# The attention front of a fused attention and gated-MLP kernel, written out as a list of small steps pinned on every engine

## Chip, core and metric

The kernel runs on one core of a Trainium2 chip. The metric is the device time of one execution in microseconds (us). The engines are TensorE (PE; its weight loads are PEld), VectorE (DVE), ScalarE (ACT), GpSimd (POOL) and SyncE (SP, which here only issues DMAs). Each engine runs its own instructions in the order in which they stand in its program, and waits on semaphores for the others.

## What is computed

```python
def _attn_ref(q, k, v):                 # q, k, v: (8, 8, 576, 64)
    scores = scale * np.matmul(q, k.transpose(0, 1, 3, 2))
    mask = (rel >= 0) & (rel < 64)      # sliding window of 64
    scores = np.where(mask, scores, -1000000000.0)
    attn = softmax(scores)              # max subtracted, sum + 1e-09
    return np.matmul(attn, v)
def _moe_ref(x, w_gate, w_val, w_out):  # x: (4608, 512), d_ff 1536
    gate = 1.0 / (1.0 + np.exp(-(x @ w_gate)))
    return (gate * (x @ w_val)) @ w_out
```

The attention output, heads side by side, is the x of the second function.

## The kernel before

The 4608 tokens are cut into 12 tiles of 384. A tile's attention is worked in four **units** (t, p): t is the tile's place in the order of work, p a pair of heads. A unit has two halves h, and in each three pieces u of 128x128. The path of a unit is:

- `load_qk`, `load_v`: three DMAs of 192, 224 and 384 KB.
- `scores` (s): 24 small matmuls (L224).
- `exponentials`: for each of six pieces, DVE adds the mask and takes the row's lowest value (L249), ACT takes the exponential (L257), for h = 0 with its row sum.
- `normalize`: for h = 1 DVE sums the rows (L270). DVE doubles the sum (L264) and inverts it (L265), POOL multiplies the half by it (L274).
- `stage_b`: three transposes on PE (pp, L328) and a copy by ACT (pT, L333) for each half.
- `stage_c`: 24 matmuls with v (oo, L358), then `x_split`: ACT writes the rounded x (L365), DVE the rest that rounding lost (L366).

Weights come from HBM as 64-bit words of 512 KB a block and are turned to float32 on the chip: **conv** i, with i = 3 j + m, where m is 0 for the gate, 1 for the value and 2 for the output weights. `conv_load` is the DMA into one of 6 raw buffers; `conv_a` is two ACT steps (L117 into one of 3 w32 buffers, L118); `conv_b` is three DVE steps (L126, L128, L130); `conv_c` is ACT's rounding (L158), DVE's rest (L159) and the stores for later use, among them the w32 buffer itself (L154). A w32 buffer is free for the next conv once L159 is done and that store has landed.

The MLP of tiles 0 and 1 is `up(t, j, 0)` (gate), `up(t, j, 1)` (value), 12 matmuls each (L394): for each p three products, of w rounded and x rounded, w rounded and x's rest, w's rest and x rounded. A `ph` result lies in one of three PSUM banks, taken in turn. ACT's tanh (L402) empties the gate's bank, DVE's product (L407) the value's; L420 and L422 split the hidden value, and `down` (L442, 9 matmuls for a j) adds it up. The order is up(0,0), up(1,0), up(0,1), down(0,0), up(1,1), up(0,2) and so on. From t = 2 on, another attention unit is put in about every 12 us. Later tiles use products of summed blocks (L619), of which most of the time consists.

The order within an engine comes from two things. The kernel's lines are put on a list of events with due times (`put`, sorted near the end), and PE's matmuls are kept in the order of that list (`pe`). On the other engines the scheduler of the framework picks the order; `issue_after(x)` puts an instruction behind x on the same engine, without a wait when it runs.

Of the kernel before, what the change touches and what calls it, by code (L numbers as in the profile page):

```python
# [26 lines left out]
def attn_ffn(ctx: ExitStack, tc: tile.TileContext, qT, kT, vN, w_gate, w_val, w_out, out, outT):  # L27
# [74 lines left out]
    def conv_load(i):  # L102
        j, m = divmod(i, KINDS)
        raw = mp.tile([P, DM], I64, name=f"raw_{m}_{j}", tag="raw", bufs=RAW)
        marks["conv_load"] = nc.sync.dma_start(out=raw, in_=w_src[m][J_AT[j]]).ins
        conv[i] = raw

    def conv_a(i):


        j, m = divmod(i, KINDS)
        raw = conv[i]
        hw = raw.bitcast(F32).rearrange("p (n two) -> p n two", two=2)[:, :, 1]
# [3 lines left out]
        nc.scalar.activation(w32, hw, AF.Copy, scale=2.0 ** -112)  # L117
        nc.scalar.activation(r32, lw, AF.Copy, scale=2.0 ** -29)  # L118
        conv[i] = (r32, w32)

    def conv_b(i):
        j, m = divmod(i, KINDS)
        r32, w32 = conv[i]
        wi = w32.bitcast(I32)
        zz = mp.tile([P, DM], I32, name=f"zz_{m}_{j}", tag="u", bufs=2)
        nc.vector.tensor_scalar(out=zz, in0=wi, scalar1=4, scalar2=1,  # L126
                                op0=ALU.logical_shift_left, op1=ALU.logical_shift_right)
        nc.vector.scalar_tensor_tensor(out=wi, in0=wi, scalar=-2 ** 31, in1=zz,  # L128
                                       op0=ALU.bitwise_and, op1=ALU.bitwise_or)
        nc.vector.tensor_add(out=wi, in0=wi, in1=r32)  # L130

    def conv_c(i):
        j, m = divmod(i, KINDS)
        _, w32 = conv.pop(i)
# [7 lines left out]
        J = J_AT[j]  # L142
        if m == 2:
            w2 = w2.rearrange("p a b h -> p a (b h)")
            hi, lo = wo[j] = w2[:, 0, :], w2[:, 1, :]
            cp = split(w32, hi, lo, nc.vector)
            wo_all[j] = w2
            wo_parts(j)
        else:
            cp = split(w32.rearrange("p (a h) -> p a h", a=2), w2[:, :, 0, :], w2[:, :, 1, :], nc.vector)  # L150
            wgv[m][j] = w2
            for name, half in (("A11", 0), ("A12", 1)) if J < NK else (("A22", 1),):
                put_part(m, J % NK, name, w2[:, half])
# [12 lines left out]
    def load_qk(t, p):
# [10 lines left out]
        nc.sync.dma_start(out=qt, in_=qT[rows, c0:c0 + TT])  # L180
        nc.sync.dma_start(out=kt, in_=kT[rows, c0:c0 + TT + BLK])
        ld[(t, p)] = (qt, kt)

    def load_v(t, p):
        i = 8 + 4 * t + p
# [5 lines left out]
        nc.sync.dma_start(out=vt, in_=vN[r0:r0 + P, :].rearrange("p (u c) -> p u c", u=UT))  # L191
# [20 lines left out]

    def scores(t, p, starts=(True,) * (2 * UP)):
# [15 lines left out]
    def softmax(t, p):  # L229
        sc = sc_of.pop((t, p))  # L230
        for h in range(2):
            exponentials(t, p, h, sc[h])
            normalize(t, p, h)

    def exponentials(t, p, h, sc):
        g0 = order[t] * UT
# [85 lines left out]

    def stage_b(t, p):
        for h in range(2):
            pt = st[(t, p, h)]
            pp = bank(t, p, f"p{h}", f"pp{h}_{t}_{p}")
            for u in range(UP):
                pe(nc.tensor.transpose(pp[:, u, :], pt[:, u, :], ident))  # L328
            if t < 2:
                pT = mp.tile([P, TT], F32, name=f"pT{h}_{t}_{p}", tag="g", bufs=4).rearrange("p (u c) -> p u c", u=UP)  # L330
            else:
                pT = pt
            cp = nc.scalar.copy(pT, pp)  # L333
            marks["pTv"] = cp.ins
            if t < 2:
                marks["pT"][NP * t + p] = cp.ins
            st[(t, p, h)] = pT

    def stage_c(t, p):
        oo = bank(t, p, "o", f"oo_{t}_{p}")  # L340
        outputs(t, p, [oo[:, u, :] for u in range(UP)])
        oo = oo.rearrange("p u c -> p (u c)")
        if t < 2:
            xs[(t, p)] = x_split(oo, f"{t}_{p}", 4 * t + p, nc.vector)
        else:
            marks["xf"] = nc.scalar.copy(xf_tile(t, p), oo).ins
# [59 lines left out]
    def gated(out, val, g):  # L406
        nc.vector.scalar_tensor_tensor(out=out, in0=g, scalar=1.0, in1=val, op0=ALU.add, op1=ALU.mult)  # L407

    def up_gate(t, j):
        gate_table(t, j, up(t, j, 0))  # L410

    def hidden_split(t, j, h32, eng):
# [7 lines left out]
        nc.vector.tensor_copy(out=h_hi, in_=h32)  # L420
        hh[(t, j)] = (h_hi, h_lo)
        return eng.tensor_sub(out=h_lo, in0=h32, in1=h_hi.bitcast(F32))  # L422

    def up_val(t, j):
        ph = up(t, j, 1)
        g = gates.pop((t, j))
        h32 = mp.tile([P, TT], F32, name=f"h32_{t}_{j}", tag="c", bufs=CB)
        gated(h32, ph, g)
        last = hidden_split(t, j, h32, nc.vector)
        if t == 0:  # L430
            marks[j] = (marks["gate"], last.ins)

    def down(t, j, i, first, last):
# [46 lines left out]
    def put_part(m, k, name, parts):  # L480
        nc.sync.dma_start(out=wd[k][N_OF[name]][:, m], in_=parts.bitcast(F32))
# [319 lines left out]
    for i, (kind, t, j) in enumerate(plan):  # L801
# [31 lines left out]
    def last_tile(t, js):  # L833
# [5 lines left out]
        for n, (j, x) in enumerate(items):  # L839
# [3 lines left out]
            put(now, 9, down, t, j, x, j == js[0], j == js[-1])  # L843
# [111 lines left out]
    events.sort(key=lambda x: (x[0], x[1]))  # L955
    for tm, _, f, a in events:
        if f in (conv_a, conv_b, conv_c):
            with ExitStack() as behind:
# [5 lines left out]
                key = j - AHEAD if m < 2 else j - 1  # L964
                early = {3: ("1_1",), 2: ("1_3",), 4: ("1_3",), 5: ("1_3",)}.get(a[0], (key,))
# [54 lines left out]
```

## Time and profile before

| | before |
|---|---|
| three runs | 946.29, 947.2, 947.6 us, median 947.2 |
| the profiled execution | span 945.2 us from first to last instruction; the median of the runs is 2.0 us more |
| PE busy | 930.8 us, 98% of the span |
| DVE, ACT, POOL busy | 713.7 (76%), 501.7 (53%), 151.2 us (16%) |

The span is the time between the first and the last instruction of one profiled execution. A busy PE isn't one at its peak: matmuls are pipelined and their ends modelled. Times below count from the start of the span. The **front** is the stretch up to about 40 us, in which the eight units of tiles 0 and 1 are worked and the first weights turned.

### The profile page before, as it was taken

To read this page: it belongs to the slowest core of one execution; us is meant where nothing else is said; L and a number is where in the kernel's file an instruction comes from. 1 tells how busy PE (TensorE), PEld (TensorE's weight loads), DVE (VectorE), ACT (ScalarE), POOL (GpSimd) and SP (SyncE) were. 2 spreads that over 40 slices of the span, in tenths; PEclk is the share of its full clock that TensorE was granted. 3 is DMA by queue.
4 is the path that set the end of the run, shared out by engine and by line. 5 is a ranking of instruction groups with operands and counts; after the bars stand their busy time and mean duration, and the time that the engine had idled before them with its cause. 6 is when DMAs were issued, how large, how long until landed. Compare 5 with 4: busy or idle time off the path is not lost.

```text
span 945.2 us, 20293 instructions
## 1 busy us (share of the span) xinstructions
PE 930.8 (98%) x7164; PEld 897.2 (95%) x7164; DVE 713.7 (76%) x1919; ACT 501.7 (53%) x1374; POOL 151.2 (16%) x232
## 2 busy tenths in 40 slices
PE   6999999999999999999999999999999999999998
PEld 5899999889999999999999999999999999999998
DVE  7999989887888975666885676796567796566882
ACT  7867676655666653545653255564155555222450
POOL 4201104605683000311100013100011100000000
PEclk9999999999999999999999999999999999999999
DMA  9899998989999989888879888889888688988364
GB/s 339 309 386 366 359 320 283 358 295 352 388 321 314 405 284 294 288 273 270 269 251 312 264 283 293 270 244 288 284 278 280 213 246 281 297 251 256 128 222 158
DMA packets 105509, 273.45 MB, mean 289 GB/s; under 512 B 11456, under 2 KB 33600, under 8 KB 105408
## 3 DMA queue, kind: packets, MB, share of 16 engines
q1 hardware_dynamic: 105408, 272.15, 85.2%
q8 instruction: 57, 0.93, 0.4%
q14 instruction: 44, 0.36, 0.1%
HBM read 220.20 MB, written 51.90 MB: 288 GB/s over the span
## 4 chain that ended last, share of the span: by engine, by line
PE 95%; DVE 2%; DMA 1%; ACT 0%; issue 0%; DVEq 0%; ACTq 0%
PE pr L619 46%; PE y L619 23%; PE ph L394 10%; PE y L442 5%; PE pp L328 3%; PE pr L358 2%; PE s L224 1%; PE oo L358 1%; PE pr L224 1%; DMA wt<-wd 1%; PE s L358 1%; DVE p L249 0%; DVE rs L264 0%; ACT p L257 0%; DVE x L366 0%; DVE rs L270 0%
## 5 line engine op out<-in xcount | busy, mean ns | idle before, releaser
L619 PE MATMUL pr<-x_T,wt 128*128 128x384 f32 x1224 | 224.5, 335 | 0.0
L619 PE MATMUL y<-h,wot 128*128 128x384 f32 x1260 | 219.9, 334 | 0.0
L619 PEld LDWEIGHTS y<-h,wot 128*128 128x128 f32 x1260 | 218.3, 188 | 0.7 <-DVE h L407 0.6
L619 PEld LDWEIGHTS pr<-x_T,wt 128*128 128x128 f32 x1224 | 212.6, 188 | 0.3 <-issue 0.3
L619 PE MATMUL pr<-x_B,wt 128*128 128x384 f32 x1008 | 188.6, 337 | 1.0 <-DMA wt<-wd 1.0
L619 PEld LDWEIGHTS pr<-x_B,wt 128*128 128x128 f32 x1008 | 174.6, 188 | 3.5 <-issue 2.1
L701 ACT CAST h<-h 128x384 fp32r<-128x384 f32 x210 | 104.3, 514 | 91.7 <-PE y L619 41.1
L274 POOL TENSOR_TENSOR p<-p,rs 128x384 f32<-128x384 f32 x76 | 69.3, 926 | 521.7 <-DVE rs L265 243.3
L702 DVE TENSOR_TENSOR h<-h,h 128x384 fp32r<-128x384 f32 x210 | 111.7, 559 | 22.0 <-ACT h L701 21.5
L257 ACT ACTIVATE p<-p,mn 128x128 f32<-128x128 f32 x288 | 110.8, 392 | 20.5 <-DVE mn L249 20.2
L402 ACT ACTIVATE g<-c 128x384 f32<-128x384 f32 x90 | 47.0, 522 | 117.7 <-DVE c L658 117.5
L394 PE MATMUL ph<-x,w 128*128 128x384 f32 x576 | 106.0, 338 | 0.1
L394 PEld LDWEIGHTS ph<-x,w 128*128 128x128 f32 x576 | 99.8, 188 | 2.5 <-issue 0.9
L629 DVE TENSOR_TENSOR c<-pr,p 128x384 f32<-128x384 f32 x60 | 33.0, 550 | 44.5 <-PE pr L619 44.5
L407 DVE SCALAR_TENSOR_TENSOR h<-g,c 128x384 f32<-128x384 f32 x90 | 50.3, 559 | 6.2 <-DVE c L658 0.5
L257 ACT ACTIVATION_READ_ACCUMULATOR p<-p,mn 128x1 f32 x264 | 49.6, 188 | 0.0
L333 ACT COPY p<-pp 128x384 f32<-128x384 f32 x80 | 34.3, 479 | 25.9 <-PE pp L328 23.1
L634 ACT COPY p<-pr 128x384 f32<-128x384 f32 x60 | 27.2, 473 | 37.0 <-PE pr L619 36.9
L629 DVE TENSOR_TENSOR u<-pr,p 128x384 f32<-128x384 f32 x60 | 33.1, 551 | 17.6 <-PE pr L619 17.6
L328 PE MATMUL pp<-ident,p 128*128 128x128 f32 x288 | 41.8, 280 | 2.0 <-POOL p L274 1.9
L619 PE MATMUL pr<-x_T,ws 128*128 128x384 f32 x216 | 40.4, 339 | 0.0
L658 DVE TENSOR_TENSOR c<-pr,p 128x384 f32<-128x384 f32 x60 | 32.9, 554 | 9.6 <-PE pr L619 9.1
(186 smaller groups left out, 1212.1 us busy)
## 6 DMA issues: line engine op xcount, KB each, us to landing
wt<-wd SPq DMA_DIRECT2D x186, 512.0 KB, 4.5
wot<-wod SPq DMA_DIRECT2D x105, 512.0 KB, 4.6
v<-in_vN_dram SPq DMA_DIRECT2D x48, 384.0 KB, 5.5
wd<-ws SPq DMA_DIRECT2D x48, 256.0 KB, 4.9
k<-in_kT_dram SPq DMA_DIRECT2D x48, 224.0 KB, 5.5
q<-in_qT_dram SPq DMA_DIRECT2D x48, 192.0 KB, 5.4
w32d<-w SPq DMA_DIRECT2D x36, 256.0 KB, 4.9
wd<-w SPq DMA_DIRECT2D x36, 256.0 KB, 5.5
```

The source lines that it names most:

```text
L257: exp = nc.scalar.activation(pt[:, u, :], pt[:, u, :], AF.Exp, bias=mn[:, u:u + 1], scale=-1.0, **sums)
L274: eng.tensor_mul(out=pt, in0=pt, in1=rs.unsqueeze(2).broadcast_to([P, UP, P]))
L328: pe(nc.tensor.transpose(pp[:, u, :], pt[:, u, :], ident))
L358: pe(nc.tensor.matmul(oo[U // 2][h * BLK:(h + 1) * BLK, U % 2 * BLK:(U % 2 + 1) * BLK], vt[:, U, h * BLK:(h + 1) * BLK], pT[h][:, U // 2, ...
L394: pe(nc.tensor.matmul(ph, l, r, start=i == 0, stop=i == len(prs) - 1))
L402: act = nc.scalar.activation(g, c, AF.Tanh)
L407: nc.vector.scalar_tensor_tensor(out=out, in0=g, scalar=1.0, in1=val, op0=ALU.add, op1=ALU.mult)
L442: pe(nc.tensor.matmul(yb[y], l, r, start=first and n == 0, stop=last and n == 2))
L619: pe(nc.tensor.matmul(ps, l, r, start=first and i == 0, stop=last and i == 2, skip_group_check=not check))
L629: marks["plus"] = nc.vector.tensor_add(out=o, in0=ps, in1=a).ins
L701: nc.scalar.copy(h2[:, 0, :], src)
L702: nc.vector.tensor_sub(out=h2[:, 1, :], in0=src, in1=h2[:, 0, :].bitcast(F32))
```

## The change

The functions of the front are cut into small named steps, and a string, FRONT, lists 330 of them: 49 loads and stores, 36 steps of PE, 98 of ACT, 131 of DVE and 16 of POOL. They are traced in this order before all other events, and each engine keeps exactly this order (`Pinned`, with SP among the engines). A step's name is two letters and its numbers: `lq`, `lv` loads, `sc` scores, `tt` L249, `ex` L257, `rd` L270, `ia` L264, `ib` L265, `mu` L274, `tr` and `cp` transposes and copy, `ou` L358, `xh`, `xl` x rounded and its rest, `ug`, `uv` the two `up`, `ut` tanh, `ud`, `uh`, `ul` L407, L420, L422; and of conv: `cl` load, `ch`, `cw` L117 and L118, `cz`, `cs`, `ca` L126, L128, L130, `cc`, `cr` L158 and L159, `ct`, `cd` stores. The list holds all eight units, up(0,0), up(1,0) but for its value's product, and conv 0 to 7. Steps that the list names are not run again by the events. All other events due before 60 are put behind the last pinned instruction of their engine. Some explicit orders go, such as the exponentials' `issue_after` to a pT copy. No instruction is added or taken away.

```diff
+FRONT = """
+lq0.0 cl0 lq0.1 lq0.2 sc0.0 lq1.0 lq0.3 ch0 tt0.0.0.1 tt0.0.0.2 cw0 lv0.1 tt0.0.0.0 tt0.0.1.1 lv0.0 sc0.1
+tt0.0.1.0 ex0.0.0.0 tt0.0.1.2 lq1.1 ex0.0.0.1 ex0.0.0.2 ex0.0.1.1 ia0.0.0 sc0.2 ib0.0.0 ex0.0.1.2 lq1.3
+tt0.1.0.1 mu0.0.0 tt0.1.0.0 ex0.0.1.0 tt0.1.0.2 ex0.1.0.1 rd0.0.1 ex0.1.0.2 lq1.2 tt0.1.1.0 tr0.0.0 ex0.1.0.0
+tt0.1.1.1 ia0.0.1 tt0.2.0.1 ex0.1.1.0 ia0.1.0 ib0.0.1 ex0.1.1.1 tt0.1.1.2 sc0.3 mu0.0.1 tt0.2.0.0 ex0.2.0.1
+tt0.2.0.2 tt0.2.1.2 lv0.2 ex0.1.1.2 tt0.2.1.0 ex0.2.0.0 ib0.1.0 tt0.2.1.1 tr0.0.1 mu0.1.0 rd0.1.1 cp0.0.0
+sc1.0 lv0.3 ex0.2.0.2 tt0.3.0.2 tt0.3.0.1 ex0.2.1.0 lv1.2 ia0.1.1 tr0.1.0 cz0 cp0.0.1 ou0.0 tt0.3.0.0 lv1.1
...
+ex1.2.1.2 rd1.1.1 cd1 cc1 tt1.3.0.1 cl7 ex1.2.0.0 rd1.2.1 cl5 ex1.2.0.1 tt1.3.0.2 cr1 uv0.0 ch3 lq2.0
+tt1.3.1.0 cw4 ia1.1.1 tt1.3.1.1 ia1.2.0 ia1.2.1 ex1.3.1.1 ib1.1.1 cz3 mu1.1.1 ch4 tt1.3.1.2 cs3 ex1.3.0.1
+ut0.0 tr1.1.1 cz4 cp1.1.0 ib1.2.1 ib1.2.0 ud0.0 cp1.1.1 mu1.2.0 ou1.1 cs4 ex1.3.1.0 ex1.3.1.2 mu1.2.1
+ex1.3.0.2 rd1.3.1 ex1.3.0.0 ia1.3.1 cw3 ia1.3.0 tr1.2.1 ib1.3.0 ib1.3.1 ca4 mu1.3.0 tr1.2.0 cw2 ca3 cd4 xh1.0
+mu1.3.1 ch2 tr1.3.0 xl1.0 cd3 cp1.2.0 cz2 ct1 tr1.3.1 cp1.2.1 cs2 ou1.2 cp1.3.0 cl9 cp1.3.1 ca2 xh1.1 cl10
+ou1.3 cc3 xl1.1 cd2 xh1.2 cr3 cc4 lv2.2 xl1.2 xh1.3 ct3 cw5 xl1.3 ug1.0 cl8 ch6 uh0.0 cr4 cc2 uv1.0 cz6 ch7
+cr2 cw6 cs6 cz7 ca6 ch5 cs7 cl12 cw7 cz5 ut1.0 ul0.0 cc6 cs5 ca7 ca5 cc7 cl13 cr6 cd6 cc5 cd7 cr7 ct2 cr5 cd5
+ct6 lv2.0 ct4 ct7 cl11
+"""
...
+    class Pinned:
...
+                ins = getattr(self.eng, op)(*a, **k)
+                if pinned[0]:
+                    tc.keep_in_program_order(ins)
+                    ends[ins.ins.engine] = ins.ins
+                return ins
...
+    def run(name, *a):
+        if (name,) + a not in taken:
+            taken.add((name,) + a)
+            steps[name](*a)
...
-                if NP * t + p - 2 in marks["pT"] and (t, p) != (1, NP - 1):
-                    behind.enter_context(tc.issue_after(marks["pT"][NP * t + p - 2]))
...
+    pinned[0] = True
+    for token in FRONT.split():
+        run(token[:2], *map(int, token[2:].split(".")))
+    pinned[0] = False
     for tm, _, f, a in events:
...
+            for ins in ends.values() if tm < 60 else ():
+                behind.enter_context(tc.issue_after(ins))
...
-                if a[0] < 2:
-                    behind.enter_context(tc.issue_after(marks["pT"][a[0] + (f is conv_c)]))
```

## Rows read from the trace of the kernel before

**Rows 1.** The head of the page: the span, each engine's busy time, and PE's busy tenths in 40 slices of 23.6 us.
```profile
span 945.2 us, 20293 instructions
PE 930.8 (98%) x7164; PEld 897.2 (95%) x7164; DVE 713.7 (76%) x1919; ACT 501.7 (53%) x1374; POOL 151.2 (16%) x232
PE   6999999999999999999999999999999999999998
```

**Rows 2.** Busy time of the engines by stretch: the sum over 0 to 40.3 us, and the stretch from 40 to 60 us (length, then busy us and instructions of PE, PEld, DVE, ACT, POOL, granted clock as a share of 2.4 GHz, DMA share, GB/s).
```profile
sum 40.30, PE 30.92 PEld 24.95 DVE 31.67 ACT 31.95 POOL 16.45; mean PE 3.86 PEld 3.12 DVE 3.96 ACT 3.99 POOL 2.06
...
40.00:60.00 20.00, 20.00 (x139) 18.90 (x134) 17.77 (x46) 16.07 (x38) 0.00 (x0) 1.00 0.94 332
```

**Rows 3.** The chain that ended last, from 36 to 54 us (start, length, engine, tile and line).
```profile
36.23 1.48 PE pp L328 x12
...
37.79 0.85 ACT pT L333 x2
...
38.69 1.67 PE oo L358 x46
40.37 8.72 PE ph L394 x48
...
51.17 2.11 PE ph L394 x12
53.28 0.82 PE s L224 x24
```

**Rows 4.** The first instructions of PE in order of time (start, length, and in brackets the idle time before and what ended it).
```profile
3.91 1.55 PE L224 MATMUL s<-k,q 64*64 64x128 f32 x24 [3.91 <-DMA k<-in_kT_dram]
6.57 2.84 PE L224 MATMUL s<-k,q 64*64 64x128 f32 x48 [1.11 <-DMA k<-in_kT_dram]
```

**Rows 5.** Two DMA issues of SP, of k for unit (0,1) and of v for (0,0) (start of issue), and under them the same two with size and us from issue to landing.
```profile
2.11 0.43 SPq L181 DMA_DIRECT2D k<-in_kT_dram  x1
...
3.53 0.43 SPq L191 DMA_DIRECT2D v<-in_vN_dram  x1
...
k<-in_kT_dram SPq DMA_DIRECT2D x1, 224.0 KB, 4.3
...
v<-in_vN_dram SPq DMA_DIRECT2D x1, 384.0 KB, 4.9
```

**Rows 6.** DVE and ACT in order of time: the first step of unit (0,1) on each, four ACT steps in a row, and the last x steps of the front.
```profile
8.79 0.28 DVE L249 CUSTOM_DVE_ANT_0 p<-s,m 128x128 f32<-128x128 f32 x1
...
9.12 0.40 ACT L257 ACTIVATE p<-p,mn 128x128 f32<-128x128 f32 x1 [1.03 <-DVE mn L249]
...
18.41 0.61 ACT L158 CAST w<-w 128x512 fp32r<-128x512 f32 x1
...
18.92 0.67 ACT L117 ACTIVATE w<-raw 128x512 f32<-128x512 f32 x1
...
19.49 0.67 ACT L118 ACTIVATE raw<-raw 128x512 int32<-128x512 uint32 x1
...
20.05 0.45 ACT L365 CAST x<-oo 128x384 fp32r<-128x384 f32 x1
...
40.34 0.85 ACT L365 CAST x<-oo 128x384 fp32r<-128x384 f32 x2
...
41.08 1.01 DVE L366 TENSOR_TENSOR x<-oo,x 128x384 fp32r<-128x384 f32 x2
```

**Rows 7.** Busy time of the engines from ACT's first step of unit (0,1) to the end of its last x step (columns as in rows 2).
```profile
9.12:41.19 32.07, 27.71 (x397) 22.19 (x390) 29.11 (x140) 29.21 (x98) 13.19 (x15) 1.00 0.95 357
```

**Rows 8.** DVE's instructions up to 45 us grouped by line (count, busy us, mean ns, idle time before them).
```profile
L264 DVE SCALAR_TENSOR_TENSOR rs<-rs 128x3 f32<-128x3 f32 x16 | 4.5, 280 | 1.0 <-ACT p L257 0.8
...
L130 DVE CUSTOM_DVE_ANT_0 w<-raw,w 128x1024 uint16<-128x1024 uint16 x5 | 3.6, 723 | 0.3
L128 DVE SCALAR_TENSOR_TENSOR w<-w,zz 128x512 int32<-128x512 int32 x5 | 3.4, 688 | 0.1
...
L126 DVE TENSOR_SCALAR zz<-w 128x512 int32<-128x512 int32 x5 | 2.1, 419 | 0.0
```

**Rows 9.** POOL's multiplications and the DVE steps beside them, in order of time.
```profile
17.20 0.69 DVE L130 CUSTOM_DVE_ANT_0 w<-raw,w 128x1024 uint16<-128x1024 uint16 x1
17.31 1.27 POOL L274 TENSOR_TENSOR p<-p,rs 128x384 f32<-128x384 f32 x1 [2.08 <-ACT p L257]
...
26.41 0.83 POOL L274 TENSOR_TENSOR p<-p,rs 128x384 f32<-128x384 f32 x1 [1.64 <-DVE rs L265]
...
26.60 0.65 DVE L264 SCALAR_TENSOR_TENSOR rs<-rs 128x3 f32<-128x3 f32 x1
```

**Rows 10.** Two stores of a w32 buffer (issue, then us from issue to landing), the waits of ACT's L117 for such stores from 41 to 140 us (total, times, longest), and DVE's product of up(1,0).
```profile
26.25 0.33 SPq L154 DMA_DIRECT2D w32d<-w  x1
...
39.81 0.32 SPq L154 DMA_DIRECT2D w32d<-w  x1
...
w32d<-w SPq DMA_DIRECT2D x1, 256.0 KB, 7.0
...
w32d<-w SPq DMA_DIRECT2D x1, 256.0 KB, 3.8
...
ACT w L117 <- DMA w32d<-w: 6.7, 6, 2.9
...
45.42 0.55 DVE L407 SCALAR_TENSOR_TENSOR h<-g,ph 128x384 f32<-128x384 f32 x1
```

More of the change, by code (lines that the diff above doesn't have):

```diff
@@ L117, in conv_a, with cz @@
[L117 to L121, printed above, removed]
+        scalar.activation(r32, lw, AF.Copy, scale=2.0 ** -29)
+        conv[i]["r32"] = r32
+    @step
+    def cz(i):
         j, m = divmod(i, KINDS)
-        r32, w32 = conv[i]
-        wi = w32.bitcast(I32)
+        wi = conv[i]["w32"].bitcast(I32)
         zz = mp.tile([P, DM], I32, name=f"zz_{m}_{j}", tag="u", bufs=2)
[L126 to L130, printed above, removed]
@@ L133, in conv_c, with cc @@
+    @step
+    def cc(i):
         j, m = divmod(i, KINDS)
-        _, w32 = conv.pop(i)
+        w32 = conv[i]["w32"]
         if m < 2 or j < 8:
@@ L211, in pieces, with sc, front_scores @@
         return [b[:, u, :] for u in range(UP)]
+    @step
+    def sc(t, p):
+        scores(t, p)
+    def front_scores(t, p):
+        run("sc", t, p)
     def scores(t, p, starts=(True,) * (2 * UP)):
@@ L229, in softmax @@
     def softmax(t, p):
+        if t < 2:
+            for h in range(2):
+                for u in range(UP):
+                    run("tt", t, p, h, u)
+                    run("ex", t, p, h, u)
+                for name in ("rd",) * h + ("ia", "ib", "mu"):
+                    run(name, t, p, h)
+            return
         sc = sc_of.pop((t, p))
@@ L233, in softmax, with mask_of, lowest @@
             normalize(t, p, h)
-    def exponentials(t, p, h, sc):
-        g0 = order[t] * UT
+    def mask_of(t, u, h):
+        key = [int((order[t] * UT + 2 * u + s) % SEQ == 0) for s in range(2)]
+        return masks[tuple(key[::-1] if h else key)]
+    def lowest(t, p, h):
         if t < 2 and (NP * t + p) % 3 == 2:
@@ L321, in stage_n, with tr, cp @@
             normalize(t, p, h)
+    @step
+    def tr(t, p, h):
+        pt = st[(t, p, h)]
+        pp = pp_of[(t, p, h)] = bank(t, p, f"p{h}", f"pp{h}_{t}_{p}")
+        for u in range(UP):
+            pe(nc.tensor.transpose(pp[:, u, :], pt[:, u, :], ident))
+    @step
+    def cp(t, p, h):
+        pp = pp_of.pop((t, p, h))
+        if t < 2:
+            pT = mp.tile([P, TT], F32, name=f"pT{h}_{t}_{p}", tag="g", bufs=4).rearrange("p (u c) -> p u c", u=UP)
+        else:
+            pT = st[(t, p, h)]
+        marks["pTv"] = scalar.copy(pT, pp).ins
+        if t < 2:
+            marks["pT"][NP * t + p] = marks["pTv"]
+        st[(t, p, h)] = pT
@@ L335, in stage_b, with ou, xh @@
-            if t < 2:
-                marks["pT"][NP * t + p] = cp.ins
-            st[(t, p, h)] = pT
+            run("tr", t, p, h)
+            run("cp", t, p, h)
+    @step
+    def ou(t, p):
+        oo = oo_of[(t, p)] = bank(t, p, "o", f"oo_{t}_{p}")
+        outputs(t, p, [oo[:, u, :] for u in range(UP)])
+    @step
+    def xh(t, p):
+        oo = oo_of[(t, p)].rearrange("p u c -> p (u c)")
+        if t < 2:
+            x2 = xs[(t, p)] = xp.tile([P, 2, TT], F32R, name=f"x_{t}_{p}", tag=f"x{4 * t + p}")
+            marks[f"{t}_{p}"] = (scalar.copy(x2[:, 0, :], oo).ins,)
+        else:
+            marks["xf"] = scalar.copy(xf_tile(t, p), oo).ins
@@ L339, in stage_c, with xl @@
+    @step
+    def xl(t, p):
+        oo = oo_of.pop((t, p)).rearrange("p u c -> p (u c)")
+        x2 = xs[(t, p)]
+        lo = vector.tensor_sub(out=x2[:, 1, :], in0=oo, in1=x2[:, 0, :].bitcast(F32))
+        marks[f"{t}_{p}"] += (lo.ins,)
     def stage_c(t, p):
-        oo = bank(t, p, "o", f"oo_{t}_{p}")
-        outputs(t, p, [oo[:, u, :] for u in range(UP)])
-        oo = oo.rearrange("p u c -> p (u c)")
+        run("ou", t, p)
+        run("xh", t, p)
         if t < 2:
-            xs[(t, p)] = x_split(oo, f"{t}_{p}", 4 * t + p, nc.vector)
-        else:
-            marks["xf"] = nc.scalar.copy(xf_tile(t, p), oo).ins
+            run("xl", t, p)
@@ L419, in hidden_split, with ul, down, dn @@
             h_lo = mp.tile([P, TT], F32R, name=f"hl_{t}_{j}", tag="hl", bufs=3)
-        nc.vector.tensor_copy(out=h_hi, in_=h32)
+        vector.tensor_copy(out=h_hi, in_=h32)
+        hh[(t, j)] = (h_hi, h_lo, h32)
+    @step
+    def ul(t, j):
+        h_hi, h_lo, h32 = hh[(t, j)]
         hh[(t, j)] = (h_hi, h_lo)
-        return eng.tensor_sub(out=h_lo, in0=h32, in1=h_hi.bitcast(F32))
+        lo = vector.tensor_sub(out=h_lo, in0=h32, in1=h_hi.bitcast(F32))
+        if t == 0:
+            marks[j] = (marks["gate"], lo.ins)
     def up_val(t, j):
[L425 to L433, printed above, removed]
+        for name in ("uv", "ud", "uh", "ul"):
+            run(name, t, j)
+    def down(t, j, i):
+        run("dn", t, j, i)
+    @step
+    def dn(t, j, i):
+        first, last = j == 0, j == NF - 1
         h_hi, h_lo = hh[(t, j)]
```

221 lines of the change are left out of this document (156 added, 65 removed).

## The prediction

> **What bounds the kernel now.** Read the head of the page first: PE is busy for 930.8 of 945.2 us, 14.4 us short of the whole, and the only slices below nine tenths are the first and the last [rows 1]. The busy times by stretch then say where the 14.4 us lie: up to 40.3 us PE is busy for 30.92, so 9.4 us are lost there, and from 40 to 60 us it is busy without a gap [rows 2]. Some 5 us are scattered over the other 900. What the front can give is therefore at most 9.4 us, and 3.9 of them pass before the first q and k are there [rows 4]; that leaves 5.5.
>
> The chain tells what ends the front. PE's last attention products follow a copy by ACT, and at 40.37 `up(1,0)` begins, behind which PE never stands still [rows 3]. But `up(1,0)` needs all four x of tile 1, and the last rest of x (DVE, L366) ends at 41.08 + 1.01 = 42.09, just when the tenth of its first twelve matmuls (8.72 / 48 = 0.18 us each [rows 3]) wants it: 40.37 + 9 x 0.18 = 42.0 [rows 3, 6]. So one event is the gate: **the last xl of tile 1, now at 42.09**. PE's work behind it is the same in both kernels, and a shift of the gate is a shift of the end, as long as nothing new stops PE later. In front of the gate PE isn't what is short: between ACT's first step of unit (0,1) and its last x step, 32.07 us, PE has 27.71 us of work, ACT 29.21 and DVE 29.11 [rows 7]. The front is a relay of ACT and DVE, each idle for only some 2.9 us of 32; the first question to the new order is what it adds to them ahead of the gate.
>
> **The change, part by part.** No instruction is added or lost, so only places count. I reckon along ACT, from its first step of unit (0,1) to its last xh, and take DVE's own sum as a bound.
>
> *Start, +0.8 us.* The list puts the raw block of conv 0, 512 KB, second on SP's queue, ahead of q and k of (0,1). k of (0,1) now lands at 2.11 + 4.3 = 6.41, v of (0,0), 800 KB further on, at 3.53 + 4.9 = 8.43: 2.5 us per 1000 KB, so 512 KB cost 1.3 us [rows 5]. The scores of (0,1) start at 6.57 + 1.3 = 7.9 instead of 6.57, and take 1.55 like those of (0,0): 9.4 [rows 4]. On the other side ACT has L117 and L118 of conv 0 ahead of its first exponential, and DVE's `ia0.0.0` waits for three exponentials ahead of `tt0.1.*`; with raw at 6.7 (96 KB behind 6.41), two conv steps of 0.57 each and the exponentials, that gives 9.6. I take 9.6 against 8.79 now, and ACT's step 0.33 behind it as now, 9.9 against 9.12 [rows 6]. Lower bound: the block, of larger rows, costs nothing, 0. What hides the price now is nothing: ACT waits for it (1.03 us idle there already).
>
> *Work moved ahead of the gate, +1.5 us on ACT.* Today L117, L118 and L158 of three convs lie in that stretch. The list has four of each (`cw0` and `ch0` come sooner still, but conv 3 and 4 are whole and conv 2 has its first two). One more of each costs, from start to start, 0.57 (18.92 to 19.49), 0.56 (to 20.05) and 0.51 (18.41 to 18.92), less the 0.1 of a fourth L117 that already reaches into the stretch [rows 6]. On DVE the three steps of conv 4 and of conv 2 come ahead of the last xl: 2 x (0.42 + 0.69 + 0.72) = 3.7 us [rows 8], less the two splitting steps of the hidden value that go behind it, about 1.4 by the nearest rows of that size: +2.3.
>
> *Idle time that goes, -2.9 us.* ACT's idle time is 32.07 - 29.21 = 2.86, DVE's 2.96 [rows 7]. A list dense enough removes all of it; that is the most there is.
>
> *Idle time that comes, +1.3 us.* First, PE is late early: behind the scores of (0,1), at 9.4, the list has s(0,2), a transpose, s(0,3), a transpose, s(1,0), a transpose, oo(0,0) and the transposes of `cp0.1.1`. At 1.55 for 24 matmuls this is done near 17.4, at the later pace (0.82 [rows 3]) about 13; ACT is at that copy at about 16.2. Between 0 and 1.2, I take 0.8: the early pace is the nearer row. Second, `ch4` wants the w32 buffer of conv 0, whose store follows `cr0`, which stands 15 us of DVE work behind 9.6 and some 1.5 us of losses: 26. The store takes 3.8 to 7.0 us [rows 10], with the two ahead of it about 32; ACT is there at about 31.5. I take 0.5 of 0 to 1.5. Such waits are known from later (6.7 us over six [rows 10]); there they hold nobody up.
>
> *Behind the gate, +0.3 us.* From the gate to `up(1,1)` PE has 51.17 - 42.09 = 9.1 us of work [rows 3, 6]. Its bank is free only when DVE's L407 of up(1,0) has run, which is at 45.42 now [rows 10] and which the list leaves out: it has to stand behind the last pinned DVE step. Between xl1.3 and that end lie 16 steps: three whole convs, two L159 and the split, at the durations of rows 8 and 0.08 less from start to start about 8.5, with L407 9.1. The cover is gone: whatever DVE waits for in that tail, PE waits too. Cost 0 to 3.2 (the spread of a store's landing, 3.8 to 7.0, since `ch6` and `ch5` take buffers that conv 3 and 2 must give up [rows 10]); I take 0.3, since the stores' queue has less in it by then, as at 39.81.
>
> *Edits at nothing.* The other moved loads and stores pass SP in an order whose landings lie ahead of need; the dropped `issue_after` costs no wait at run time. DVE's work finished early (conv 5 to 7) gains nothing, since PE has no gap there that it would fill.
>
> **Sum:** 0.8 + 1.5 - 2.9 + 1.3 + 0.3 = +1.0 us, the gate near 42.8 and the span 946.2. With the 2.0 us by which the runs' median stands above this span: 948.2. A change of 0.2% is 1.9 us, about what a measurement of this kernel can tell from none, so this is no change that would show.
>
> **DVE and POOL.** DVE's L264 begun at 26.60, 0.19 us into a POOL multiplication, took 0.65 against a mean of 0.28 and ended with it; the multiplication begun at 17.31 inside a DVE step took 1.27 instead of 0.83 [rows 8, 9]. So a step of one holds up the other. The Trainium skill (SBUF — State Buffer, section "SBUF: two separate sides") says that the two share a port pair under an exclusive lock, which whoever starts first keeps for its whole instruction, and that DVE steps with two SBUF inputs need it. That speaks against this change, since it moves such steps in among the multiplications; the trace agrees in both directions. By that rule the sum would be that of rival C.
>
> **Rivals.** *A, faster.* ACT never idles and the raw block costs nothing at the start: 1.5 - 2.9 = -1.4; and a tighter start of the later tiles takes another 1 of the 5 us that PE loses elsewhere. For it: every engine's order is free of the scheduler's guesses. Against: the extra work on both engines ahead of the gate. About 944.8. Chance 0.20.
>
> *B, slower: PE waits for the bank at up(1,1).* One place, L407 of up(1,0), behind 16 pinned steps. It decides once DVE's tail is more than about 1 us longer than PE's 9.1; at the late landing it gives 1.0 + 2.9 = +3.9, in the middle +2.5: 949.7. Against: stores at that time may land as quickly as at 39.81. Chance 0.15.
>
> *C, slower: DVE is the bound of the front.* Start 0.8, work 2.3, idle -3.0, so +0.1 and whatever DVE loses. Four more conv steps with two SBUF inputs than now stand among the multiplications; POOL is busy 0.41 of the stretch [rows 7], and a hit costs half of 0.83: 0.7. With 2 of the 3 us of idle time still there the gate moves by +2.8: 950.0. It decides from 1.8 us of DVE losses. Chance 0.17.
>
> *D, the order is nearly the old one.* The scheduler's order might be close to the list; then within 0.5 of 947.2. Against: conv 1, 3 and 4 plainly move. It is part of the 0.48 that no change that shows has in all.
>
> **How the numbers follow.** Faster 0.20 (A), the same 0.48 (the sum with its smaller bounds, and D), slower 0.32 (B and C). The likeliest case gives 948.2, by itself 945.8 to 949.0. The range leaves out the better half of A at the bottom and, at the top, B and C where they add up: 944.4 to 951.0.
>
> **What would show it.** In the new profile: the first L249 of (0,1) at about 9.6; ACT's L117 with a wait for a w32 store near 31; the last xl between 42 and 44, and `up(1,0)` beginning at 40.5 to 41.5; a PE wait before `up(1,1)` for DVE's L407 or none; PE's busy time up to the gate as now. The prediction is wrong if the last xl comes before 41 (ACT's work per step is then less than I took, or the idle time is all gone), or if PE shows new gaps of over 2 us behind the gate.

## The result and the profile after

The changed kernel takes 952.3 us (median of six runs, 949.6 to 955.0) against 947.4 for the kernel before beside it: ratio 1.0054, 95% interval 1.0039 to 1.0068. It is slower by some 5 us. The forecast was 948.2, between 944.4 and 951.0.

The head of its page (span; busy time of the engines; PE's busy tenths and granted clock in 40 slices of 23.8 us) has to be held against [rows 1]:

```profile
span 950.5 us, 20265 instructions
PE 930.8 (98%) x7164; PEld 897.2 (94%) x7164; DVE 712.7 (75%) x1919; ACT 501.6 (53%) x1374; POOL 153.1 (16%) x232
PE   6889999999999999999999999999999999999998
...
PEclk9999999999999999999999999999999999999999
```

PE's work is the same 930.8 us, and the span is 5.3 us longer: what came in is idle time, and a little slow clock that the slices are too coarse to show. Two slices have fallen from 9 to 8: the second, 23.8 to 47.5 us, which holds the end of the front, and the third, 47.5 to 71 us, which lies behind it. Most of the loss is in the third, as the starts of PE's matmuls show further down. The chain that ended last, from the gate on (start, length, engine, tile and line; every step of the list is recorded at L125, the helper in `Pinned`, so there one goes by tiles; L568 is `up`, L644 `down`), against [rows 3]:

```profile
41.22 8.18 DMA w32d<-w
...
49.48 0.66 ACT w L125
50.15 0.56 ACT raw L125
50.70 0.38 ACT g L125
...
51.13 3.72 PE ph L568 x12
54.85 2.08 PE y L644 x9
56.93 2.11 PE ph L568 x12
```

Before, PE ran through here without a break. Now the end of the kernel hangs on the store of a w32 buffer, issued at 41.22. The waits from 41 to 100 us (us in total, times, longest) name who is held up:

```profile
ACT w L125 <- DMA w32d<-w: 7.1, 4, 3.9
DVE zz L125 <- ACT w L125: 6.9, 4, 2.9
...
PEld ph L568 <- ACT g L125: 3.6, 1, 3.6
...
PE ph L568 <- ACT g L125: 3.3, 1, 3.3
```

And the timeline from 36 us gives the order on the queue and on the engines:

```profile
39.88 0.65 SPq L125 DMA_DIRECT2D raw<-in_moe_w_gate_dram  x1
...
40.62 0.51 SPq L125 DMA_DIRECT2D raw<-in_moe_w_val_dram  x1
...
41.22 0.41 SPq L125 DMA_DIRECT2D w32d<-w  x1
...
41.29 6.55 PE L568 MATMUL ph<-x,w 128*128 128x384 f32 x36
...
41.75 1.22 DVE L125 TENSOR_TENSOR x<-oo,x 128x384 fp32r<-128x384 f32 x2
...
49.48 0.66 ACT L125 ACTIVATE w<-raw 128x512 f32<-128x512 f32 x1 [3.95 <-DMA w32d<-w]
...
51.13 3.72 PE L568 MATMUL ph<-x,w 128*128 128x384 f32 x12 [3.29 <-ACT g L125]
```

Read it from the bottom. PE wants to begin the value half of `up(0,1)` at 47.84 (41.29 + 6.55). The `ph` banks are taken in turn, so it needs the one that the gate of `up(1,0)` filled, and ACT's tanh (`ut1.0`, tile g) has to empty that. The tanh stands on ACT behind `ch5` and `cw7` of the list. `ch5` wants the w32 buffer of conv 2, whose store `cd2` stands on SP behind `cl9` and `cl10`, two blocks of 512 KB. From issue to landing, of the issues between 40 and 42 us:

```profile
raw<-in_moe_w_val_dram SPq DMA_DIRECT2D x1, 512.0 KB, 8.1
...
w32d<-w SPq DMA_DIRECT2D x1, 256.0 KB, 8.2
```

Before, the store issued at 39.81 landed in 3.8 us [rows 10]. The stretches show why (length; busy us of PE, PEld, DVE, ACT, POOL; granted clock, DMA share, GB/s), first the kernel before, from 36 and 40 us, then the new one:

```profile
36.00:40.00 4.00, 3.33 (x64) 2.89 (x60) 3.59 (x7) 3.31 (x8) 0.83 (x1) 1.00 0.53 204
40.00:45.00 5.00, 5.00 (x38) 4.71 (x33) 4.38 (x9) 5.00 (x11) 0.00 (x0) 1.00 0.74 221
```

```profile
36.00:40.00 4.00, 2.34 (x26) 1.70 (x28) 3.93 (x9) 3.12 (x8) 2.56 (x3) 1.00 0.88 312
40.00:45.00 5.00, 4.89 (x63) 4.73 (x58) 4.69 (x10) 4.75 (x11) 0.00 (x0) 1.00 1.04 345
```

The DMA engines were half idle ahead of the gate; now they are full. The clock behind the wait, by PE's own row of the new kernel (length; busy us; granted clock, DMA share, GB/s):

```profile
50.73:54.15 3.42, 3.02 (x9) 0.50 0.50 136
```

After the 3.29 us in which PE stood, its granted clock is 0.50, the 1.2 GHz level, for 3.4 us, so the twelve matmuls took 3.72 us where twelve take 2.11 in the chain above: 1.6 us more.

By the starts of PE's matmuls in the traces (us; "151st" is the 151st `up` matmul, "product" the first matmul of the summed blocks; one profiled execution of each kernel):

| kernel | up(1,0) | value of up(0,1) | up(1,1) | 151st | product | span |
|---|---|---|---|---|---|---|
| before | 40.30 | 46.85 | 51.01 | 68.38 | 209.07 | 945.2 |
| after | 41.29 | 51.13 | 56.77 | 74.14 | 214.89 | 950.5 |
| e1_store_first | 41.24 | 48.92 | 53.20 | 73.07 | 215.12 | 950.6 |
| e2_tanh_first | 42.84 | 49.20 | 55.99 | 74.99 | 216.08 | 952.0 |
| e3_tanh_rest_first | 41.79 | 48.17 | 53.63 | 71.08 | 212.19 | 947.1 |
| e4_no_tail | 43.28 | 49.64 | 53.80 | 71.17 | 212.95 | 947.8 |
| e5_filled | 41.97 | 48.33 | 52.49 | 69.86 | 212.67 | 947.4 |
| e6_conv_behind | 40.81 | 47.16 | 51.45 | 70.90 | 211.48 | 947.7 |
| e7_start | 41.75 | 48.10 | 52.26 | 69.63 | 211.87 | 948.1 |
| e8_all | 39.23 | 45.60 | 49.89 | 69.28 | 211.55 | 947.4 |
| e12_four_w32 | 41.63 | 48.04 | 52.20 | 69.82 | 214.08 | 951.2 |
| e13_four_w32_no_tail | 42.16 | 48.54 | 52.70 | 70.08 | 214.32 | 952.1 |
| b2_four_w32 | 40.36 | 46.88 | 51.24 | 74.89 | 218.90 | 957.2 |

So of the 5.76 us that the new kernel is behind at `up(1,1)`, 0.99 were there at the gate, 3.29 are the wait and some 1.5 the low clock. By the first product it is 5.82, by the end 5.3: hardly anything moves behind that. The 0.99 is the least certain of these numbers: the lists of the changed kernel, e2, e3 and e4 are the same up to the gate, and yet it came at 41.29, 42.84, 41.79 and 43.28. In e2 and e4, the late ones, PE ran at the low clock for 3.4 us ahead of it.

### The profile page after: what moved, and what is told of

It reads as the page before. It is cut to its first block, busy times and chain, and to the rows that moved or that the text cites. A ratio compares the mean times of both kernels' runs of the same rounds, so it can differ in the third digit from the quotient of the medians.

```text
span 950.5 us, 20265 instructions
## 1 busy us (share of the span) xinstructions
PE 930.8 (98%) x7164; PEld 897.2 (94%) x7164; DVE 712.7 (75%) x1919; ACT 501.6 (53%) x1374; POOL 153.1 (16%) x232
## 4 chain that ended last, share of the span: by engine, by line
PE 91%; DVE 3%; DMA 2%; issue 0%; ACT 0%; SPq 0%; DVEq 0%; ACTq 0%
PE pr L821 46%; PE y L821 23%; PE ph L568 10%; PE y L644 3%; PE pp L484 3%; PE pr L540 2%; PE s L335 1%; DMA w32d<-w 1%; PE pr L335 1%; PE s L540 1%; DVE w L125 1%; DMA wa<-w32d 1%; DMA out_dram<-yo 0%; PE oo L540 0%; DVE x_T L816 0%
## 5 line engine op out<-in xcount | busy, mean ns | idle before, releaser
L430 POOL TENSOR_TENSOR p<-p,rs 128x384 f32<-128x384 f32 x60 | 55.4, 940 | 505.8 <-DVE rs L125 236.9
L568 PE MATMUL ph<-x,w 128*128 128x384 f32 x576 | 107.5, 341 | 3.9 <-ACT g L125 3.3
L125 ACT ACTIVATE g<-c 128x384 f32<-128x384 f32 x90 | 47.0, 522 | 117.6 <-DVE c L860 111.6
L568 PEld LDWEIGHTS ph<-x,w 128*128 128x128 f32 x576 | 101.1, 190 | 6.7 <-ACT g L125 3.6
L413 ACT ACTIVATE p<-p,mn 128x128 f32<-128x128 f32 x240 | 93.5, 392 | 15.7 <-DVE mn L408 15.7
L831 DVE TENSOR_TENSOR c<-pr,p 128x384 f32<-128x384 f32 x60 | 33.0, 551 | 44.0 <-PE pr L821 44.0
L125 DVE SCALAR_TENSOR_TENSOR h<-g,c 128x384 f32<-128x384 f32 x90 | 50.4, 560 | 5.9
L125 ACT COPY p<-pp 128x384 f32<-128x384 f32 x80 | 34.4, 479 | 26.9 <-PE pp L484 26.1
L413 ACT ACTIVATION_READ_ACCUMULATOR p<-p,mn 128x1 f32 x240 | 45.1, 188 | 0.0
L484 PEld LDWEIGHTS pp<-ident,p 128*128 128x128 f32 x288 | 33.9, 141 | 7.7 <-POOL p L125 4.6
L821 PE MATMUL pr<-x_T,ws 128*128 128x384 f32 x216 | 40.5, 339 | 0.2 <-DVE u L831 0.2
```

Source lines behind the costliest of these rows:

```text
L125: ins = getattr(self.eng, op)(*a, **k)
L430: eng.tensor_mul(out=pt, in0=pt, in1=rs.unsqueeze(2).broadcast_to([P, UP, P]))
L568: pe(nc.tensor.matmul(ph, l, r, start=i == 0, stop=i == len(prs) - 1))
L821: pe(nc.tensor.matmul(ps, l, r, start=first and i == 0, stop=last and i == 2, skip_group_check=not check))
L831: marks["plus"] = nc.vector.tensor_add(out=o, in0=ps, in1=a).ins
```

## The experiments

The theory: the loss is a chain, late store, `ch5`, tanh, bank, and the order of the list's **tail** behind the gate makes it. The rival: the front itself is worse, and the tail only shows it.

**Moving one step.** e1 puts the store ahead of the loads, e2 the tanh ahead of `ch5`, e3 in addition DVE's last split ahead of conv 5's DVE steps.

```diff
 e1: -... cp1.3.0 cl9 cp1.3.1 ca2 xh1.1 cl10 ou1.3 cc3 xl1.1 cd2 xh1.2
     +... cp1.3.0 cp1.3.1 ca2 xh1.1 ou1.3 cc3 xl1.1 cd2 cl9 cl10 xh1.2
 e2: -... ca6 ch5 cs7 cl12 cw7 cz5 ut1.0 ul0.0 cc6
     +... ca6 ut1.0 ch5 cs7 cl12 cw7 cz5 ul0.0 cc6
 e3: +... ca6 ut1.0 ch5 cs7 cl12 cw7 ul0.0 cz5 cc6
```

> One step moved in the list: the store of conv 2's w32 buffer (cd2) goes ahead of the two 512 KB loads cl9 and cl10. Theory T (the 5 us are made behind the gate: PE waits 3.3 us for the tanh of up(1,0), which stands on ACT behind conv 5's L117, which waits for that store; and PE then runs its next 12 matmuls at half clock, 1.6 us): the store lands some 2.6 us sooner, PE's wait falls to under 1 us and the slow stretch goes; 947.5 to 949 us. Rival R1 (the front itself is late, DVE and POOL hold each other up, and PE would stand elsewhere if not here): 951 to 952.5. Rival R2 (the slow clock comes by itself): the wait goes, the slow stretch of 1.6 us stays, 949 to 950.

> One step moved on ACT: the tanh of up(1,0) (ut1.0) ahead of conv 5's L117 (ch5). T: PE's wait of 3.3 us at the value half of up(0,1) goes, but ch5 still waits for the store until about 49.5, and behind it on DVE stand ul0.0 (until 51.1; down(0,0) wants it at 49.7) and the product of up(1,0) (until 55; up(1,1) wants its bank at 52): PE waits there instead, 3 us in all: 950 to 951. R1: 952. If the tanh alone was the cause: 947.5.

> As e2, and ul0.0 ahead of conv 5's first DVE step (cz5). T: no wait at up(0,1) nor at down(0,0), but the product of up(1,0) still stands behind the list's last DVE step, so PE waits about 3 us before up(1,1): 950 to 951. If only the order of tanh and rest mattered: 947.5. R1: 952.

Measured: 952.5 (1.0039 [1.0025, 1.0054]), 953.1 (1.0054 [1.0038, 1.0070]) and 952.0 us (1.0044 [1.0031, 1.0056]); none is told from the changed kernel. All three lie above the theory's ranges and at or near the rival's numbers, so by their times alone the rival would have won; only the traces speak for the theory. The waits of e1, PE's from 41 to 100 us, then ACT's and DVE's from 41 to 62 us; under them SP's issues around the store, and the store from issue to landing:

```profile
PE pp L483 <- POOL p L429: 1.2, 1, 1.2
PE ph L567 <- ACT g L124: 1.2, 1, 1.2
PE ph L567 <- DVE h L124: 0.5, 1, 0.5
```

```profile
ACT w L124 <- DMA w32d<-w: 4.6, 3, 2.5
```

```profile
DVE zz L124 <- ACT w L124: 5.4, 3, 4.5
```

```profile
43.58 0.32 SPq L732 DMA_DIRECT2D a<-w32d  x1
...
43.99 0.38 SPq L124 DMA_DIRECT2D w32d<-w  x1
...
44.47 0.38 SPq L124 DMA_DIRECT2D raw<-in_moe_w_gate_dram  x1
```

```profile
w32d<-w SPq DMA_DIRECT2D x1, 256.0 KB, 3.2
```

The store now landed in 3.2 us, but it was issued 2.8 us later: a load that the list doesn't name (L732, of a stored w32 block) now stood ahead of it on SP and held SP for 3.6 us. The list fixes the order of its own steps only; others can stand between them. So the store landed at 47.19 instead of 49.40, 2.2 us sooner, and PE's wait for the tanh fell by 2.1, from 3.3 to 1.2; the clock stayed at the upper level. That is the chain as described. But the two loads went out at 44.47 and 44.94, over 4 us later than in the changed kernel, DVE stood 4.5 us for a conv step, by the 151st matmul the gain of 3.6 us at `up(1,1)` was down to 1.1, and by the first product it was gone. So e1 moved more than the store. In e2 the same wait appears one stage further on, at `up(1,1)`, with the low clock behind it (PE's timeline, then PE's row of a stretch):

```profile
55.99 3.91 PE L567 MATMUL ph<-x,w 128*128 128x384 f32 x12 [2.20 <-DVE h L124]
```

```profile
56.20:59.61 3.41, 3.41 (x12) 0.50 1.05 398
```

In e3 PE waited 1.1 us at the same place, with the clock up; its profiled execution was the fastest of eight (948.9 us), so what the 952 us of the others hold isn't shown. Moving the step that suffered from the wait didn't remove it here: the next one queued there took it over.

**Leaving the tail to the events.** e4 cuts the list behind `xl1.3`.

```diff
-... xh1.3 ct3 cw5 xl1.3 ug1.0 cl8 ch6 uh0.0 ... ct7 cl11
+... xh1.3 ct3 cw5 xl1.3
```

> The list ends with xl1.3; the 40 steps behind it are left to the events and the scheduler as before the change. T: the gate stays at about 43 (0.9 later than before the change), PE has no wait of over 0.5 us behind it, no slow stretch: 947.5 to 948.5. R1: the front costs the most, 950.5 to 952. R2: 949 to 950.

Measured: 949.25 us, 1.0015 [1.0003, 1.0027]. PE has no wait between 41 and 100 us. So the tail costs some 3 of the 4.9 us, and 1.6 stay, 0.3 to 2.6 by the interval (the kernel before had 947.65 in these runs). The time lies between the theory's range and the rival's, in that of R2, the low clock that comes by itself; the profile does show 3.4 us at the low clock, from 39.55, ahead of the gate and behind gaps of 0.9 us at most.

**What is left.** e5 keeps PE busy with 18 transposes of the identity that nothing reads, in the three gaps ahead of the gate; e6 takes the conv steps of blocks 2 and 4 out of the list; e7 loads conv 0 behind the q and k loads of tile 0 and turns it later; e8 is all three. All stand on e4.

```diff
 e5: +... ou1.1 fl0 cs4 ... tr1.2.0 fl1 cw2 ... tr1.3.0 fl2 xl1.0 ...
     +        for _ in range(6):
     +            pe(nc.tensor.transpose(f[:, :P], ident, ident))
 e6: -ch2 cw2 cz2 cs2 ca2 cd2 ch4 cw4 cz4 cs4 ca4 cc4 cd4
 e7: -lq0.0 cl0 lq0.1 lq0.2 sc0.0 lq1.0 lq0.3 ch0 ...
     +lq0.0 lq0.1 lq0.2 sc0.0 lq1.0 lq0.3 cl0 ... ch0 cw0 cp0.0.0
```

> The list cut behind xl1.3 as in e4_no_tail, and three times six transposes of the identity into a bank that nobody reads, placed on PE where it waits for POOL (behind oo(1,1) and the transposes of (1,2) and (1,3)): 18 extra matmuls that are no part of the computation. Theory C (what is left of the loss in e4_no_tail, 1.6 us, and its spread are a fall of PE's clock to half near 39 us, after a stretch in which PE stands still often): no fall in the profile, the tenth matmul of up(1,0) at 43.0 instead of 45.0, 947.3 to 948.3. Rival (the clock falls by chance, whatever PE does; or the gate itself costs): still a fall in the front in half of the runs, 949 to 950.

> The list cut behind xl1.3, and in it the steps of conv 2 and 4 between loads and the gate (ch, cw, cz, cs, ca, cc, cd) left out, so that the events place them behind the gate. Term of the sum under test: extra conv work ahead of the gate, 1.5 us on ACT, 2.3 on DVE. If it holds, the gate (tenth matmul of up(1,0)) comes 1 to 1.5 us sooner than in e4_no_tail with the same clock, near 41.7; conv 4's rest may then be late for the value half of up(0,1), a wait of 0 to 1: 947.5 to 949. If conv work ahead of the gate costs nothing (DVE and ACT had room), the gate stays at 43.

> The list cut behind xl1.3; the raw block of conv 0 goes behind q and k of (0,3) on SP's queue, and its two ACT steps ahead of the first pT copy. Term under test: the start. The scores of (0,1) then begin at 6.6 instead of 8.4 and ACT's first step of (0,1) at 9.2 instead of 10.8, but 1.1 us of conv work moves behind it: the gate 0.3 to 0.6 sooner than in e4_no_tail, 948.5 to 949. If the start alone sets the gate: 1.7 sooner.

> e5, e6 and e7 together (the extra matmuls again no part of the computation). If the three act on the same chain and add: gate near 41, no fall of the clock, no wait behind it: 945.5 to 946.8, faster than the kernel before. If one takes the place of another: 947 to 948.

Measured: 949.1 (1.0013 [1.0004, 1.0023]), 950.0 (1.0027 [1.0017, 1.0036]), 949.6 (1.0022 [1.0013, 1.0032]) and 949.5 us (1.0024 [1.0013, 1.0034]). PE's row of the stretch around the gate in e4, then in e5, and after it PE's only wait from 41 to 180 us in e8:

```profile
39.50:43.00 3.50, 3.09 (x45) 0.51 1.12 357
```

```profile
39.50:43.00 3.50, 3.36 (x60) 1.00 1.04 358
```

```profile
PE y L647 <- DVE w L122: 1.8, 1, 1.8
```

With the fillers the clock stayed up and the gate of the profiled run came 1.3 us sooner than in e4, yet the median moved by 0.2; the time is the one that the rival had. That the fillers kept the clock up isn't shown, since it also stayed up without them in the profiled runs of the changed kernel, e1, e3 and e6. e6, e7 and e8 took longer than any time expected of them and aren't told from e4. In e7 the scores of (0,1) began at 6.19 instead of 8.44, and the gate still came only at 41.75. In e8 the gate came 1.1 us sooner than in the kernel before, the only order that did so. But at 61 us PE stood 1.8 us because the rest of conv 5 (tile w) came late for `down(0,1)`, and from 190 to 200 us it stood another 1.5 us, where the kernel before stood 0.1. The theory that the remaining loss is the later gate fell here: the early gate was given back, first to late weights, as in e6, and then to waits for an attention unit.

**A fourth w32 buffer.** e12 is the list unchanged, with room made by smaller pools; b2 is the kernel before with the same pools; e13 is e12 with the list cut as in e4.

```diff
-    RAW, W32 = 6, 3
+    RAW, W32 = 6, 4
-    WB, WOB, CB, EXTRA = 7, 7, 3, 5
+    WB, WOB, CB, EXTRA = 7, 7, 2, 5
-    sm = ctx.enter_context(tc.tile_pool(name="sm", bufs=8))
+    sm = ctx.enter_context(tc.tile_pool(name="sm", bufs=5))
```

> The kernel after with four w32 buffers in place of three (room for it by two `c` buffers in place of three and five `sm` buffers in place of eight); the list and its order are unchanged. If the buffer that waits for the late store is what costs PE its 3.3 us: `ch5` takes the fourth buffer and waits for no store, the tanh comes some 4 us sooner, PE doesn't stand ahead of the value half of up(0,1) and its clock doesn't fall, so up(1,1) begins near 52.0 in place of 56.8, and the time is 952.3 - 4.8 = 947.5 (946 to 949) if that stays won. If instead the loss behind the gate lies in the pinned tail whatever its buffers (DVE's 16 steps ahead of up(1,1)'s bank): 951 to 953. Each is to be read against the kernel before with the same buffers, which runs beside it.

> The control: the kernel before with the same buffers (four w32, two `c`, five `sm`). By the theory of the store: before lost nothing to w32 buffers behind the gate, so at most 1 us faster, 946.5 to 948.5. If fewer `c` and `sm` buffers cost something of their own, it is slower, and what it loses is to be taken off the run beside it. If the fourth buffer helps any order alike: faster by the same 3 to 5 us as the changed kernel.

> Four w32 buffers as in the run beside it, and the list cut behind the last `xl` of tile 1. With three buffers this cut gave 949.3. By the theory of the store the cut is then worth nothing more: the same as the full list with four buffers within 1 us. If the order of the tail costs something besides the store, the cut is 1.5 to 3 us faster than the full list with four buffers.

Measured: 953.0 (1.0056 [1.0043, 1.0069]), 958.8 (1.0122 [1.0106, 1.0139]) and 954.1 us (1.0066 [1.0054, 1.0078]). e12's time is the one that its rival had, and the control is 5.8 us slower than e12 itself. The smaller pools cost far more than expected, and not the same in both, so the times settle nothing; the traces do. From the timeline of e12, PE from the gate on; its row of the stretch from 50.73 us; and PE's one wait between 41 and 100 us in b2:

```profile
41.63 8.65 PE L567 MATMUL ph<-x,w 128*128 128x384 f32 x48
```

```profile
50.73:54.15 3.42, 3.42 (x19) 1.00 1.01 379
```

```profile
PE pp L328 <- POOL p L274: 3.2, 1, 3.2
```

With a fourth buffer `ch5` waits for no store, and the same list runs its 48 matmuls in one piece and at full clock, and `up(1,1)` begins at 52.20, 4.6 us sooner than with three buffers and 1.0 behind the control: the wait for the late store is shown as the cause of PE's wait, and the low clock went with it. That e13 isn't faster than e12 agrees: apart from the store, the tail's order showed no cost. What the pools cost lies elsewhere: from the last `up` matmul to the first product, 33.0 us before and 33.1 after, but 35.8 to 35.9 in all three; and b2's wait with the lower clock behind it. In the stretch ahead of the first product PE's scores wait 1.8 us for ACT in each of the three, with the low clock behind it; in e12 (PE's timeline, then PE's row of a stretch):

```profile
184.26 1.55 PE L334 MATMUL s<-k,q 64*64 64x128 f32 x22 [1.84 <-ACT xf L124]
```

```profile
186.00:187.00 1.00, 1.00 (x3) 0.50 0.98 386
```

**Cutting the list earlier.** The list reaches `up(0,0)` at 26.2 us, the kernel before at 27.6. e14, e15 and e16 end it behind `ug0.0`, behind `uv0.0` and behind `xh0.0` (which is the first x of tile 0 and stands ahead of both: e16 is the earliest cut, not the latest as its expectation has it).

```diff
 e14: -... ct0 xl0.3 ug0.0 ex1.2.0.2 ...     +... ct0 xl0.3 ug0.0
 e15: -... cr1 uv0.0 ch3 ...                 +... cr1 uv0.0
 e16: -... ou0.1 xh0.0 ia0.2.1 ...           +... ou0.1 xh0.0
```

> The list cut behind the first matmuls of up(0,0); all that follows it comes from the events again. The list begins up(0,0) at 26.2 us, the kernel before at 27.6, and yet the list's gate is 0.8 us later; so what is lost ahead of the gate is lost between 26 and 41 us. If the list's second half is what loses it, this is the best of the cuts: gate at or ahead of 40.3, 945.5 to 948.0, no slower than before. If the loss comes from the first half (conv work left over, buffers and loads in an order that the events can't use), it stays at 949 to 950.5 as with the cut behind the last `xl`.

> The list cut behind the value half of up(0,0), some 4 us later than the run beside it. If the loss ahead of the gate builds up step by step through the second half: between the run beside it and the cut behind the last `xl` (949.25), so 947 to 949. If it lies in the last steps alone (transposes, copies and x of tile 1): the same as the run beside it.

> The list cut ahead of the first rounded x of tile 1, some 5 us of steps before the gate. If the loss lies in the last steps (the copies and x of tile 1, with the conv steps of blocks 2 and 3 between them): 947 to 948.5. If those last steps are as good as what the events do: 949 to 950, as with the cut behind the last `xl`.

Measured: 954.1 (1.0071 [1.0058, 1.0085]), 959.5 (1.0129 [1.0115, 1.0142]) and 968.3 us (1.0222 [1.0208, 1.0236]); `up(1,0)` began at 45.59, 50.16 and 57.73. All miss their expectations. PE's largest wait from 24 to 45 us in e14 and in e15:

```profile
PE oo L531 <- ACT pT L116: 6.4, 4, 2.7
```

```profile
PE oo L533 <- ACT pT L118: 8.6, 2, 5.4
```

The attention units left to the events come late behind a pinned beginning, and the granted clock was 0.50 in or behind such waits for 6.8 us in e14, 10.2 in e15 and 20.5 in e16, so these runs don't place the remaining 1.6 us; it stays open. They do show that a gate 5.3, 9.9 and 17.4 us late ends 5.8, 12.9 and 20.7 us late.

## Why the prediction was wrong

**The gate: right in sum, partly by luck.** The last xl ended at 41.75 + 1.22 = 42.97, forecast 42.8 (42.09 and the terms ahead of the gate, 0.7), and `up(1,0)` began at 41.29, inside 40.5 to 41.5. The start was under-sized by 0.9 us, and smaller errors the other way made up for most of it. From the timeline after, DVE's first L249 and ACT's first step of unit (0,1) and two POOL multiplications late in the front; then the stretch from that step to the end of the last xh; against [rows 6, 9, 7]:

```profile
10.04 0.29 DVE L125 CUSTOM_DVE_ANT_0 p<-s,m 128x128 f32<-128x128 f32 x1
...
10.79 0.40 ACT L125 ACTIVATE p<-p,mn 128x128 f32<-128x128 f32 x1
...
36.64 2.39 POOL L125 TENSOR_TENSOR p<-p,rs 128x384 f32<-128x384 f32 x2 [0.47 <-DVE rs L125]
```

```profile
10.79:42.38 31.59, 26.75 (x402) 21.06 (x395) 31.16 (x142) 30.47 (x100) 14.97 (x16) 1.00 0.95 345
```

- *Start:* L249 at 10.04 (forecast 9.6), ACT 1.67 late instead of 0.8.
- *Work ahead:* ACT's busy time rose by 30.47 - 29.21 = 1.3 (forecast 1.5), DVE's by 2.1 (2.3).
- *Idle time:* ACT kept 1.1 of 2.9 us, DVE only 0.4 of 3.0. The prediction took all 2.9 off ACT and put 1.3 back, 1.6 off in all; measured 1.7 off. Its parts came otherwise: the 0.8 for the pT copy is there (0.75), but at 39.72 and not early, and the wait of `ch4` for a store didn't come.
- *No term:* the last xl ended 0.6 us behind the last xh instead of 0.9, which hid another 0.3 of the late start.

So DVE is now the bound of the front, as rival C said; but the gate came out +0.9, not +2.8, since the list left DVE next to no idle time. The holds between DVE and POOL exist (1.2 us for each of these two multiplications where one took 0.83 [rows 9]), but over the whole stretch the mean multiplication rose only from 0.88 (13.19 / 15 [rows 7]) to 0.94 us (14.97 / 16), and DVE's busy time by no more than the moved work. The exclusive lock of the Trainium skill (SBUF — State Buffer, "SBUF: two separate sides") agrees with those rows; what it would have made of the time, rival C, didn't follow.

**Behind the gate: the step that failed.** The term "+0.3 us", between 0 and 3.2, measured 4.8. Its mechanism was the right one, a conv of the tail waiting for the buffer of conv 2, and three things in it were wrong:

- *The landing.* "the stores' queue has less in it by then, as at 39.81": the row was taken from an order in which the DMA engines were half idle. In the list two loads of 512 KB stand right ahead of `cd2`, and the upper bound of 7.0 us was passed at 8.2.
- *The place.* The prediction followed the bank to L407 on DVE and to `up(1,1)`. The first bank that PE needs again is the gate's, emptied by the tanh on ACT one stage sooner, and `ut1.0` stands behind `ch5`, the very step that waits. The list, on record with the prediction, shows this.
- *The low clock.* No term stood for it: 1.5 us on top of the wait.

With 3.3 + 1.5 in place of its 0.3 the sum is 1.0 - 0.3 + 4.8 = +5.5 and 952.7, against 952.3 measured. Rival B, a PE wait for a `ph` bank in the tail, was nearest in mechanism, though it had the wrong bank; its 949.7, and C's 950.0, were too low. The sign by which the prediction called itself wrong, new PE gaps of over 2 us behind the gate, is the one that came.

**Work finished early.** That DVE's work on conv 5 to 7, finished early, "gains nothing" isn't contradicted: from `up(1,1)` to the first product the changed kernel gained nothing on the kernel before. The reverse did show: where e6 and e8 put conv work later, PE waited 1.8 us for it.

## What to carry to other kernels

When an order is pinned, follow every buffer that is freed by a DMA: look at what stands ahead of that DMA on its queue in the new order, and at everything queued behind the waiting instruction on its engine, and stop at the first of them that PE needs. A landing time belongs to the load of the DMA engines at that moment and can't be carried to an order that loads them otherwise. Where a pinned list ends matters: here the list that ended at the gate lost 1.6 us instead of 4.9, those that ended sooner lost 6 to 20, and none of the lists tried beat the kernel without one. Count conv or prefetch work that is pushed behind a gate as due again: in e6 and e8 PE stood for it some 20 us later.

## What the runs showed of the hardware

Behind stands of PE of 3.3 us (changed kernel), 2.2 us (e2) and 3.2 us (b2) the granted clock was 0.50; behind the 1.2 us of e1 it did not fall. Stands of nearly the same length went either way: 1.84, 1.76 and 1.75 us in e12, e13 and b2 had the low clock behind them, 1.81 and 1.75 us in e6 and e8 had not. Ahead of the gate, with gaps of 0.3 to 1.1 us, it fell in the profiled runs of e2, e4 and e7 and not in those of the changed kernel, e1, e3, e12 and e13, whose gaps are alike: there the same pattern gave either level.

A 256 KB store landed in 3.2 us in e1 (DMA share 0.36 from 43 to 46 us), in 3.8 us before the change (0.53 and 0.74 around it) and in 8.2 us in the changed kernel, behind two loads of 512 KB (1.04).
